# Inverse 640-point stage by residues modulo 5, and slabs 12 and 13 without block products, in a fused spectral-filter and gated-FFN kernel

## The chip, the cores and the metric

One core of a Trainium2 chip. The metric is the device time of one execution in microseconds. TensorE (PE) multiplies matrices into PSUM; VectorE (DVE), ScalarE (ACT) and GpSimd (POOL) do the rest of the arithmetic; SyncE (SP) issues most transfers. Each engine works through its own list of instructions in order and waits on semaphores for the others.

## The reference

```python
xn = layernorm(x)                                   # x: 2048 x 640, bf16
X = rfft2(xn) * (w_r + 1j * w_i)                    # 2048 x 321 frequencies
s = irfft2(X, s=(2048, 640)).astype(bfloat16)
g = silu((gelu(xn @ w_gate) * (xn @ w_up)) @ w_down)  # 640 -> 1536 -> 640
return x + s * g
```

So there are two branches: a spectral filter (a 2048-point transform over the rows, a 640-point one over the columns, both ways) and a gated FFN; their results are multiplied.

## The kernel before

The 2048 rows are cut into 16 slabs of 128 rows (`NS = 16`). Row k of slab n1 is row 16 k + n1, so that the 2048-point transform falls into 128-point matmuls (with `Tfwd`, `Tinv`) and a 16-point part between slabs. The FFN runs over four groups g of four slabs (512 rows).

**What sets the order.** The program is recorded by hand. `back` is the list of backbone pieces, 144 places long; `put(s, f, ...)` hangs a piece of other work behind place s. The engines' lists follow this order. The backbone is the FFN: `ffn_piece` (L809, five matmuls of up to 512 columns, once for the gate, once for the up product; the gate is evacuated by ScalarE as `ge`, L814, and the product by VectorE into `UT`, L816), then the down product. The down product is either direct (`down_third`, L946, 24 matmuls of 320 columns for each slab) or by block products after Strassen and Winograd (`product`, L903, seven products of six matmuls for two slabs, with sums of operands on VectorE in `u_sum`, L884, and sums of results, L910). Groups 1 and 2 (`STR`) use block products throughout; group 3 uses them for its first two slabs, 12 and 13, at places 132 to 137, and the direct form for slabs 14 and 15. The FFN of group 2 ends at place 95, its products take places 96 to 107, the FFN of group 3 places 108 to 131, and its down stage 132 to 143. `gated` applies the SiLU (by ScalarE's table for groups 0 and 3, by a tanh on ScalarE and an operation on VectorE for 1 and 2).

**The spectral branch.** `slab_S1` and `slab_D` transform forward; the result goes through DRAM (`ZDR`) and comes back turned as `B2`. Eleven **bursts** (places 67 to 90, `BURSTS`) do the 16-point parts and the multiplication with the filter: `s2_in` makes `px` with 64 x 64 matmuls (L649), ScalarE copies it to `xs` (L657), VectorE multiplies it by W1 and W2 into `RZ` (L661); `s2_out`, one burst later, makes `pu` (L674), ScalarE copies it in two pieces (L681), even and odd frequencies apart, into a tile that goes to DRAM (`UDR`, L684). A burst covers three of sixteen row pairs and 162 or 159 of the 321 frequencies.

`load_V` (place 91) brings the result back as V, [row, slab, 2 x 321], in two pairs of transfers, slabs 0 to 3 and 4 to 15 (L699). Then, for each slab, `slab_S1i` (L730): five matmuls of 128 columns against `Tinv`, evacuated by one ScalarE copy (L732). Their operands are five blocks of 128 frequencies; four are slices of V, the fifth is put together beforehand by VectorE in `gather` (L709, two copies for a batch of slabs).

**The inverse 640-point stage** takes three slabs as a group (`DG`; the sixth group is slab 15 alone), groups seven places apart. `group_Di` calls `d_group`: for each slab four matmuls of 160 columns on 128 rows (L573) and four of 160 columns on 32 rows, in the four row strips of the array (L577), for the fifth block. It yields sums over even and odd frequencies, real and imaginary. ScalarE evacuates them with their scale (L755, 960 elements), VectorE forms sum and difference of even and odd parts (`group_cs`, L761, two operations), and then the two mirrored halves of the output (`group_Y`, L770 and L772, two operations). `finish` multiplies by the gate (L788), adds x (a transfer with accumulation on POOL's queue for slabs 0 to 11, L790; VectorE for the others, L792) and writes the output (L793).

PSUM: `psB` is two buffers of two banks each, used in turn by px, pu, slab_S1i and the inverse stage; `psA` is two buffers each for `psg` and `psu`.

Of the kernel before, what the change touches and what calls it, by code (L numbers as in the profile page):

```python
# [76 lines left out]
def build(nc, env):  # L77
# [71 lines left out]
    FI = consts.tile([P, 5, LH], BF16)  # L149
# [91 lines left out]
    lint = gtile([LH], INT32)  # L241
    nc.gpsimd.iota(lint, pattern=[[1, LH]], base=0, channel_multiplier=0)
# [10 lines left out]
    ftm = gtile([5, LH], FP32)  # L253
# [49 lines left out]
    kc = []  # L303

    def fwd_consts():
        cq = affine("cq", h_f, -320.0, 320.0)
# [4 lines left out]
        kc.append(cq)  # L311
        ab.extend([(a_m, b_0), (a_m, b_1), (a_m, b_2), (a_m, b_3), (a_y, None)])
# [3 lines left out]
    def inv_consts(part):  # L316
        if part == 0:
            for k, c in enumerate((0.0, 4.0, 2.0)):
                inv_src[k] = affine(f"i_{k}", pf, 4.0, c)
            kc.append(affine("hk", h_f, -2.0, 1.0))  # L320
        else:
            o = [affine(f"o_{k}", pf, 2.0, c) for k, c in enumerate((320.0, 2.0, 321.0, 1.0))]
            i_0, i_1, i_2 = (inv_src[k] for k in range(3))
            ab.extend([(i_0, o[0]), (i_1, o[1]), (i_2, o[2]), (i_2, o[3])])

    def inv_rest():
        cq, hk = kc
        l_s, l_k, l_r, i_r, o_r = (c1(n) for n in ("l_s", "l_k", "l_r", "i_r", "o_r"))
        for out, in0, s1, s2 in ((l_s, s_f, 2.0, 256.0), (l_k, h_f, 2.0, l_s), (l_r, hk, hi_f, l_k),
                                 (i_r, l_r, 2.0, 0.0), (o_r, l_r, 1.0, cq)):  # L330
            nc.gpsimd.tensor_scalar(out=out, in0=in0, scalar1=s1, scalar2=s2, op0=ALU.mult, op1=ALU.add)
        ab.append((i_r, o_r))
# [28 lines left out]
    fv = gtile([10, LH], FP32)  # L361

    def ft_v(g):
        if g < 5:
            parts = [(0, TW, meo[:, g // 2])] if g < 4 else [(0, 66, mys), (66, TW, mys)]
        else:
            parts = [(0, LH, lint)]
# [4 lines left out]
    FW = (TW, LH)  # L372
# [194 lines left out]
    def d_group(lhs, T, w):  # L567
        ps = [psB.tile([P, 2, 512], FP32, tag="b", name=f"pd{b}") for b in range(2)]
        n = len(lhs)
        out = [[ps[g // 2][:, g % 2, a * w:(a + 1) * w] for g in range(4)] for a in range(n)]  # L570
        for a in range(n):
            for g in range(4):
                nc.tensor.matmul(out[a][g], lhsT=lhs[a][:, g, :], rhs=T[:, g, 0:w], start=(a == 0), stop=False)  # L573
        for a in range(n):
            for g in range(4):
                r = slice(32 * g, 32 * g + 32)
                nc.tensor.matmul(out[a][g], lhsT=lhs[a][r, 4, :], rhs=T[r, 4, 0:w], start=False, stop=(a == n - 1))  # L577
        return [t[:, :, 0:n * w].rearrange("p k (a m) -> p a k m", a=n) for t in ps]

# [50 lines left out]
    WB = LH + 1  # L630
    BURSTS = [(h0, 3, l0, w) for h0 in range(0, 15, 3) for l0, w in ((0, WB), (WB, L - WB))]
# [8 lines left out]
    def s2_in(b):  # L640
# [3 lines left out]
        for lo in range(2):  # L644
            r = slice(64 * lo, 64 * lo + 64)
            for hh in range(2):
                for i, j, kind in s2_tiles(b, lo, hh):
# [3 lines left out]
                                     stop=(j == n))  # L651

# [11 lines left out]
    def s2_out(b):  # L664
# [3 lines left out]
        for q, NM in enumerate((N1, N2)):  # L668
            for hh in range(2):
                r = slice(64 * hh, 64 * hh + 64)  # L670
                for lo in range(2):
                    for i, j, kind in s2_tiles(b, lo, hh):
                        ps = pu[64 * lo:64 * lo + 64, hh, i * w:j * w].rearrange("p (h l) -> p h l", l=w)
                        nc.tensor.matmul(ps, lhsT=NM[r, kind, 0:64], rhs=pp[q][r, lo, i:j, :],  # L674
                                         start=(q == 0 and i == 0), stop=(q == 1 and j == n))
        ut = st_b["u"][:, (h0 // 3 + 1) % 2, 0:2 * n, :]
        us = ut.rearrange("p (h k) l -> p k h l", k=2)
        pv = pu[:, :, 0:n * w].rearrange("p k (h l) -> p k h l", l=w)
        for m in range(2):
            c0 = m * LH + l0 // 2  # L680
            nc.scalar.copy(out=us[:, :, :, c0:c0 + (w + 1 - m) // 2], in_=pv[:, :, :, m:w:2])  # L681
        if l0 + w == L:
            for lo in range(2):
                nc.sync.dma_start(out=rows(UDR, lo, h0, h0 + n), in_=turned(ut, lo, 0, n))  # L684
# [5 lines left out]
    VO = (0, L + 1, LH, L + 1 + HD)  # L690
# [13 lines left out]
    def gather(i):  # L704
# [3 lines left out]
        for k, c0, w in ((0, 0, LH), (1, L + 1, HD)):  # L708
            nc.vector.tensor_copy(out=vr.rearrange("p n (b k i) -> p n b k i", b=2, k=2)[:, :, :, k, :],  # L709
                                  in_=V[:, :, c0:c0 + 2 * w].rearrange("p n (b c) -> p n b c", b=2)[:, :, :, P:HD])  # L710
# [30 lines left out]
    eobuf, csbuf = (w1f[:, o:o + 6 * D].rearrange("p (s x) -> p s x", s=2) for o in (4 * D, 10 * D))  # L741

    def quad(buf, i):
        n = DG[i][1]
        return buf[:, i % 2, 0:n * D].rearrange("p (q k a n) -> p q k a n", q=2, k=2, a=n)

    def group_Di(i):
        n0, n = DG[i]
        py = d_group([st_c.pop(n0 + a) for a in range(n)], FI, HD)
        eo = quad(eobuf, i)  # L750
        silu = [(n0 + a) // 4 in BY_SILU for a in range(n)]
        edges = [0] + [a for a in range(1, n) if silu[a] != silu[a - 1]] + [n]
        for b in range(2):
            for a0, a1 in zip(edges, edges[1:]):
                nc.scalar.activation(out=eo[:, b, :, a0:a1].rearrange("p k a n -> p a k n"), in_=py[b][:, a0:a1],  # L755
                                     func=ACT.Copy, scale=(2.0 if silu[a0] else 1.0) / (S * D))

    def group_cs(i, q):
        eo, cs = quad(eobuf, i), quad(csbuf, i)
        flat = "p k a n -> p (k a n)"  # L760
        nc.vector.tensor_tensor(out=cs[:, q].rearrange(flat), in0=eo[:, 0].rearrange(flat),  # L761
                                in1=eo[:, 1].rearrange(flat), op=(ALU.add, ALU.subtract)[q])

    def group_Y(i, q):
        n0, n = DG[i]
        cs = quad(csbuf, i)
        Y = st_c["Y"](n0, n).rearrange("p a (h n) -> p a h n", h=2)
        C, Z = (cs[:, :, k].rearrange("p h a n -> p a h n") for k in range(2))
        if q == 0:
            nc.vector.tensor_tensor(out=Y[:, :, :, 0:HD], in0=C, in1=Z, op=ALU.add)  # L770
        else:
            nc.vector.tensor_tensor(out=Y[:, :, ::-1, 319:159:-1], in0=C, in1=Z, op=ALU.subtract)  # L772
# [65 lines left out]
    def gated(g, j, k, ph, late=False):  # L838
# [19 lines left out]
        else:  # L858
# [5 lines left out]
          for k, b in (((1, 0), XG[:, 0, :]), ((1, 1), RX[:, 0, :]), ((2, 0), XG[:, 0, :]), ((2, 1), SB), ((3, 0), XG[:, 0, :]))}  # L864
# [29 lines left out]
    def product(g, a, i):  # L894
# [12 lines left out]
        if a == 0 and i in (1, 2, 3) and g in STR:  # L907
# [79 lines left out]
    for g in range(4):  # L987
# [76 lines left out]
    for g, at in ((1, 56), (2, 92), (3, 128)):  # L1064
        put(at, u_sum, nc.vector, g, 0, 0, TB)
        if g in STR:
            put(at + 1, u_sum, nc.vector, g, 1, 0, TB)
# [24 lines left out]
    for b in range(len(BURSTS)):  # L1092
        put(sb + AT[b], s2_in, b)
        if b > 0:
            put(sb + AT[b], s2_out, b - 1)
    put(sb + 23, s2_out, len(BURSTS) - 1)
# [3 lines left out]
    for i, at in enumerate((vs0 - 1, vs0, vs0 + 6, vs0 + 15, vs0 + 24)):  # L1100
# [3 lines left out]
    for i, (n0, n) in enumerate(DG):  # L1104
        a = vs0 + 7 * i
# [56 lines left out]
```

## Time and profile before

| | us |
|---|---|
| median of three runs | 196.37 (195.82 to 196.56) |
| the profiled execution, device time | 197.07 |
| its span | 195.2 |
| granted TensorE clock over the span | 1.00 |

The span is the part of the execution in which the engines work; 1.87 us of the profiled execution lie around it. The page gives, for each engine, the busy time and the number of instructions, and a chain of work followed back from the last instruction: whatever released each step is the step before. A group of instructions is shown as line, engine, operation, output <- inputs, shapes and count, then busy us and mean ns of one, then the idle time just before them and what ended it. In a row of the chain stand start, length and what ran. Durations of matmuls overlap, so their rate is read from start to start or from the chain.

### The profile page before, as it was taken

What the parts mean: (1) busy time and instruction counts of PE and PEld (TensorE: products, weight loads), DVE (VectorE), ACT (ScalarE), POOL (GpSimd) and SP (SyncE); (2) the same over time, 40 slices, a digit from 0 to 9 for tenths busy, and PEclk for the clock granted to TensorE, in tenths of its full rate; (3) what the DMA queues carried; (4) which work ended last, traced back from release to release, by engine and by line L of the source; (5) the groups of instructions that cost most, each with busy time, mean ns of one, the idle gap of its engine ahead of it and who ended that gap; (6) DMA issues with size and microseconds to landing.
All of it is one profiled execution on the core that took longest, in us unless ns stands there. A gap on an engine that the chain in (4) does not pass through costs nothing.

```text
span 195.2 us, 4162 instructions
## 1 busy us (share of the span) xinstructions
PE 187.4 (96%) x1496; PEld 115.6 (59%) x1511; DVE 154.5 (79%) x379; ACT 126.6 (65%) x224; POOL 50.5 (26%) x80
## 2 busy tenths in 40 slices
PE   7899999999999999999999999999999999999992
PEld 5788854767555566576533333456765555556772
DVE  7887888989799869899965756587888657587993
ACT  4668567866977877525697787524675757465651
POOL 4448688998030200000000000000003250404100
PEclk9999999999999999999999999999999999999999
DMA  6999999968899999269955233459400836575623
GB/s 167 302 333 358 368 306 170 152 116 259 215 157 175 196 221 230 69 169 234 172 118 116 74 101 101 115 144 288 131 3 2 164 75 150 119 143 125 136 88 85
DMA packets 39989, 32.44 MB, mean 166 GB/s; under 512 B 12960, under 2 KB 38048, under 8 KB 39840
## 3 DMA queue, kind: packets, MB, share of 16 engines
q1 hardware_dynamic: 36176, 27.91, 60.3%
q0 software_dynamic: 1824, 3.28, 10.0%
q10 hardware_dynamic: 1968, 0.98, 1.9%
q8 instruction: 12, 0.20, 0.5%
q14 instruction: 9, 0.07, 0.1%
HBM read 19.03 MB, written 7.88 MB: 138 GB/s over the span
## 4 chain that ended last, share of the span: by engine, by line
PE 80%; DMA 10%; SPq 3%; DVE 3%; ACT 2%; issue 1%; DVEq 0%; ACTq 0%
PE psu L809 25%; PE psg L809 24%; PE psg L946 5%; PE psg L903 4%; PE psu L946 4%; DMA B<-ZDR 4%; PE psu L903 3%; DMA VY<-UDR 2%; PE pz L563 2%; PE pd L573 2%; SPq L624 2%; PE pv L730 2%; PE pd L594 2%; PE pu L674 2%; DMA Tfwd<-Tinv 1%
## 5 line engine op out<-in xcount | busy, mean ns | idle before, releaser
L809 PE MATMUL psu<-XG,Wu 128*128 128x512 bf16 (+2 forms) x285 | 60.4, 342 | 0.4 <-issue 0.3
L809 PE MATMUL psg<-XG,Wg 128*128 128x512 bf16 (+2 forms) x280 | 60.0, 341 | 0.7 <-issue 0.2
L816 DVE TENSOR_TENSOR UT<-psu,ge 128x512 bf16<-128x512 f32 (+2 forms) x58 | 34.4, 594 | 15.1 <-PE psu L809 12.3
L814 ACT ACTIVATE ge<-psg 128x512 bf16<-128x512 f32 (+2 forms) x58 | 30.3, 523 | 23.2 <-PE psg L809 22.5
L809 PEld LDWEIGHTS <-Wu 128*128 128x128 bf16 x290 | 26.1, 98 | 22.5 <-issue 3.4
L809 PEld LDWEIGHTS <-Wg 128*128 128x128 bf16 x290 | 26.5, 98 | 20.2 <-issue 0.2
L790 POOL DMA_DIRECT2D VY<-in_A_x_dram x12 | 10.6, 1035 | 95.3 <-PE psu L809 74.3
L661 DVE TENSOR_TENSOR RZ<-xs,W 128x972 bf16<-128x972 bf16 (+2 forms) x22 | 13.3, 648 | 9.8 <-ACT xs L657 9.5
L903 PEld LDWEIGHTS <-UT 128*128 128x128 bf16 x150 | 14.3, 98 | 6.1 <-issue 0.2
L946 PEld LDWEIGHTS <-UT 128*128 128x128 bf16 x156 | 14.4, 98 | 5.0
L599 ACT CAST RZ<-pd 128x660 bf16<-128x660 f32 x16 | 11.3, 706 | 5.6 <-PE pd L596 5.5
L189 DVE BATCH_NORM_STATS2 st<-X 128x6 f32<-128x320 bf16 x32 | 14.0, 476 | 0.4 <-DMA X<-in_A_x_dram 0.4
L755 ACT ACTIVATE W<-pd 128x960 bf16<-128x960 f32 (+2 forms) x14 | 10.0, 778 | 5.0 <-PE pd L577 5.0
L732 ACT CAST W<-pv 128x640 bf16<-128x640 f32 x16 | 11.0, 688 | 3.3 <-PE pv L730 3.1
L681 ACT CAST RX<-pu 128x486 bf16<-128x486 f32 (+4 forms) x22 | 12.3, 560 | 0.3
L946 PE MATMUL psg<-Wd,UT 128*128 128x320 bf16 (+1 forms) x84 | 11.8, 288 | 0.0
L565 ACT CAST GEN<-pz 128x640 bf16<-128x640 f32 x16 | 11.2, 698 | 0.6 <-PE pz L563 0.6
L657 ACT CAST xs<-px 128x972 bf16<-128x972 f32 (+2 forms) x11 | 10.3, 936 | 1.6 <-PE px L649 1.4
L761 DVE TENSOR_TENSOR W<-W 128x960 bf16<-128x960 bf16 (+1 forms) x12 | 7.0, 599 | 4.3 <-ACT W L755 4.3
L946 PE MATMUL psu<-Wd,UT 128*128 128x320 bf16 (+1 forms) x72 | 10.3, 291 | 0.0
L207 POOL TENSOR_TENSOR rst<-ve,mhalf 128x1 f32<-128x1 f32 (+1 forms) x6 | 5.5, 913 | 11.6 <-DVE ve L205 11.6
L903 PE MATMUL psu<-Wd,UT 128*128 128x320 bf16 x48 | 7.8, 300 | 0.0
(207 smaller groups left out, 295.7 us busy)
## 6 DMA issues: line engine op xcount, KB each, us to landing
ZDR<-RZ SPq DMA_DIRECT2D x16, 160.5 KB, 4.5
UDR<-RX SPq DMA_DIRECT2D x10, 240.8 KB, 3.0
B<-ZDR SPq DMA_DIRECT2D x8, 240.8 KB, 5.2
W<-UDR SPq DMA_DIRECT2D x2, 963.0 KB, 9.4
X<-in_A_x_dram SPq DMA_DIRECT2D x3, 640.0 KB, 10.4
Wd<-in_B_w_down_dram SPq DMA_DIRECT2D x1, 1920.0 KB, 14.7
VY<-in_A_x_dram POOLq DMA_DIRECT2D x12, 160.0 KB, 4.0
out_dram<-VY SPq DMA_DIRECT2D x12, 160.0 KB, 3.1
```

The costliest lines, as they stand in the source:

```text
L189: nc.vector.bn_stats(out=st_n[n1][:, k, :], in_=X[:, n1, 320 * k:320 * k + 320])
L565: nc.scalar.copy(out=Zt[n1], in_=pz)
L599: nc.scalar.copy(out=zd.rearrange("p c (q e) -> p c q e", e=10), in_=pd[:, :, 0:330].rearrange("p c (e q) -> p c q e", q=33))
L661: nc.vector.tensor_tensor(out=pp[-1], in0=xs, in1=WT[:, :, h0:h0 + n, l0:l0 + w], op=ALU.mult)
L681: nc.scalar.copy(out=us[:, :, :, c0:c0 + (w + 1 - m) // 2], in_=pv[:, :, :, m:w:2])
L732: nc.scalar.copy(out=vs, in_=pv)
L790: nc.gpsimd.dma_start(out=Y, in_=xv[:, n1, sl], accum_op=ALU.add)
L809: nc.tensor.matmul(ps, lhsT=WT[:, c, t * P:(t + 1) * P], rhs=xnT[g][:, c, c0:c1_], start=(c == 0), stop=(c == 4))
L814: nc.scalar.activation(out=ges[t], in_=ps, func=ACT.Gelu_apprx_tanh)
L816: nc.vector.tensor_tensor(out=UT[:, t, c0:c1_], in0=ps, in1=ges[t], op=ALU.mult)
L903: nc.tensor.matmul(ps, lhsT=lhs[:, t, :], rhs=rhs[:, t, :], start=(t == 0), stop=(t == 5))
L946: nc.tensor.matmul(ph, lhsT=UT[:, t, j * P:(j + 1) * P], rhs=Wd[:, t, c0:c1_], start=(t == 0), stop=(t == NT - 1))
```

## The change

In the inverse stage the frequencies are now ordered by their residue modulo 10: the copies out of `pu` write each residue as a run of 32 columns, in the order 8, 6, 4, 2, 0, then frequency 320, then 5, 7, 9, 1, 3. The two slices of 128 columns at 0 and at 193 then hold the frequencies that aren't multiples of 5, even and odd, and the 65 between them the multiples of 5. The part of the output that comes from multiples of 5 repeats every 128 columns; the other part sums to nothing over the five positions n, n + 128, ... So the matmuls make 128 instead of 160 columns of each sum, the missing 64 columns of each half are the negated sum of the other four blocks of 64, and the repeating part is added to all five blocks of 128 at the end.

- **Bursts.** Widths 160 and 161. VectorE copies residues 1 and 3 out of `pu` (and frequency 320 in every second burst), ScalarE residues 0 to 8 even and 5, 7, 9 in two copies. VectorE's copy comes ahead of the burst's multiplications, ScalarE's behind the copy of px.
- **Inverse stage.** `group_Di` is gone; `slab_Di` makes five matmuls of 128 columns for each slab, two or more places behind its slab_S1i, and ScalarE evacuates 640 elements. VectorE makes two sums (768 elements for three slabs) and two half outputs (768); `group_rest` is new: VectorE sums blocks twice (768, 384), ScalarE writes the negated sum (384), VectorE adds the repeating part (1920).
- **Order.** Groups are six places apart, gathers stand at places 97, 98, 103, 111 and 120 (97, 98, 104, 113 and 122 before), slab_S1i(0) at 100 (99).
- **Slabs 12 and 13** use `down_third`; their u_sum is gone.
- The constants for the inverse cosines and sines are made from other affine steps, 128 columns each instead of 161.

```diff
-    WB = LH + 1
-    BURSTS = [(h0, 3, l0, w) for h0 in range(0, 15, 3) for l0, w in ((0, WB), (WB, L - WB))]
+    WB = LH
+    BURSTS = [(h0, 3, l0, w) for h0 in range(0, 15, 3) for l0, w in ((0, HD), (HD, WB))]
...
-        for m in range(2):
-            c0 = m * LH + l0 // 2
-            nc.scalar.copy(out=us[:, :, :, c0:c0 + (w + 1 - m) // 2], in_=pv[:, :, :, m:w:2])
+        m, nq = l0 // 10, w // 10
+        for r0, ni, c0, copy in (((1, 2, HD + 97, nc.vector.tensor_copy),),
+                                 ((0, 5, P, nc.scalar.copy), (5, 3, HD + 1, nc.scalar.copy)))[part]:
+            step = -32 if r0 == 0 else 32
+            out = bass.AP(us.tensor, us.offset + c0 + m, [list(us.ap[d]) for d in (0, 2, 1)] + [[step, ni], [1, nq]])
+            src = bass.AP(pv.tensor, pv.offset + r0, [list(pv.ap[d]) for d in (0, 2, 1)] + [[2, ni], [10, nq]])
+            copy(out=out, in_=src)
...
+    def s2_step(b):
+        px = s2_in(b) if b < len(BURSTS) else None
+        pu = s2_out(b - 1) if b else None
+        if b:
+            s2_sort(b - 1, pu, 0)
+        if px is not None:
+            s2_mul(b, px)
+        if b:
+            s2_sort(b - 1, pu, 1)
...
-    def group_Di(i):
+    def slab_Di(n1):
+        i = n1 // 3
+        vs = st_c.pop(n1)
+        pd = psB.tile([P, 5, P], FP32, tag="b", name="pd")
+        for g in range(5):
+            nc.tensor.matmul(pd[:, g, :], lhsT=vs[:, g, :], rhs=FI[:, g, :], start=True, stop=True)
+        nc.scalar.activation(out=parts(eobuf, i, 5)[:, :, n1 - DG[i][0], :], in_=pd, func=ACT.Copy,
+                             scale=(2.0 if n1 // 4 in BY_SILU else 1.0) / (S * D))
...
+    def group_rest(i, q):
+        n0, n = DG[i]
+        Y = halves(i)
+        u = ubuf[:, 0:n * 256].rearrange("p (a h b e) -> p a h b e", h=2, b=2, e=64)
         if q == 0:
+            Yb = Y.rearrange("p a h (b e) -> p (a h) b e", e=64)
+            nc.vector.tensor_tensor(out=u.rearrange("p a h b e -> p (a h) b e"), in0=Yb[:, :, 0:2], in1=Yb[:, :, 4:2:-1],
+                                    op=ALU.add)
+        elif q == 1:
+            nc.vector.tensor_tensor(out=u[:, :, 0], in0=u[:, :, 0], in1=u[:, :, 1, ::-1], op=ALU.add)
+        elif q == 2:
+            nc.scalar.activation(out=Y[:, :, :, P:P + 64], in_=u[:, :, 0], func=ACT.Copy, scale=-1.0)
         else:
+            Yt = st_c["Y"](n0, n).rearrange("p a (t e) -> p a t e", t=5)
+            nc.vector.tensor_tensor(out=Yt, in0=Yt, in1=parts(eobuf, i, 5)[:, 4].unsqueeze(2).to_broadcast([P, n, 5, P]),
+                                    op=ALU.add)
...
-        if g == 3:
-            for k in range(6):
-                back.append((run,) + tuple((product, g, 0, i) for i in range(k * 7 // 6, (k + 1) * 7 // 6)))
-        for j in range(2 if g == 3 else 0, 4):
+        for j in range(4):
...
-    for i, at in enumerate((vs0 - 1, vs0, vs0 + 6, vs0 + 15, vs0 + 24)):
+    for i, at in enumerate((vs0 - 1, vs0, vs0 + 5, vs0 + 13, vs0 + 22)):
         put(at, gather, i)
...
-        a = vs0 + 7 * i
+        a = vs0 + 6 * i
         for k in range(n):
-            put(a + ((1, 2, 4)[k] if n == 3 else 1), slab_S1i, n0 + k)
-        d = a + 6 if n == 3 else a + 4
-        put(d, group_Di, i)
...
+            put(a + (2, 3, 5)[k], slab_S1i, n0 + k)
+            put(a + (4, 6, 7)[k], slab_Di, n0 + k)
+        d = a + (7 if n == 3 else 4)
+        for k, it in enumerate(((group_cs, 0), (group_cs, 1), (group_Y, 0), (group_Y, 1), (group_rest, 0),
+                                (group_rest, 1), (group_rest, 2), (group_rest, 3))):
+            put(min(d + (1, 1, 2, 2, 3, 3, 5, 6)[k], LAST), it[0], i, it[1])
         for k in range(n):
-            put(min(d + (5 + k if n == 3 else 2), vs0 + 41), finish, n0 + k)
+            put(min(d + 7 + k, LAST), finish, n0 + k)
```

More of the change, by code (lines that the diff above doesn't have):

```diff
@@ L565, in slab_S1 @@
         nc.scalar.copy(out=Zt[n1], in_=pz)
[L567 to L578, printed above, removed]
     DG = [(n0, min(3, NS - n0)) for n0 in range(0, NS, 3)]
@@ L758, in group_cs @@
[L758 to L768, printed above, removed]
[L769 to L772 removed]
+        return buf[:, i % 2, 0:g * n * P].rearrange("p (g a n) -> p g a n", g=g, a=n)
```

111 lines of the change are left out of this document (57 added, 54 removed).

## The prediction

> **What bounds the kernel now.** I read the head of the page and its chain of waits, then busy time by stage, then the chain in order of time, and last the timeline and the groups kept apart by shape.
>
> ```profile
> span 195.2 us, 4162 instructions
> PE 187.4 (96%) x1496; PEld 115.6 (59%) x1511; DVE 154.5 (79%) x379; ACT 126.6 (65%) x224; POOL 50.5 (26%) x80
> PE 80%; DMA 10%; SPq 3%; DVE 3%; ACT 2%; issue 1%; DVEq 0%; ACTq 0%
> ```
>
> TensorE is busy 96% of the span and carries 80% of the chain. By stage (busy us follow the length: PE, PEld, DVE, ACT, POOL):
>
> ```profile
> core 0: us, PE busy (x) PEld busy (x) DVE busy (x) ACT busy (x) POOL busy (x), PEclk, DMA share, GB/s
> 97.00:124.00 27.00, 26.18 (x192) 10.35 (x194) 17.19 (x30) 22.31 (x37) 0.00 (x0) 1.00 0.40 93
> 124.00:134.20 10.20, 9.75 (x64) 5.26 (x65) 6.90 (x19) 3.44 (x7) 0.00 (x0) 1.00 0.71 181
> ...
> 145.00:177.30 32.30, 32.01 (x239) 17.52 (x242) 23.25 (x47) 20.26 (x33) 7.94 (x9) 1.00 0.54 109
> 177.30:185.00 7.70, 7.70 (x80) 5.66 (x79) 6.87 (x16) 5.06 (x7) 2.62 (x3) 1.00 0.61 120
> ```
>
> The bursts (97 to 124) and all the inverse stage (from 134) have TensorE full at clock 1.00; only around the loads of V (124 to 134) does it stand, 0.45 us. VectorE has 9 of 32 us free in the middle of the inverse stage. So a matmul removed there is worth its time, as long as the two evacuating engines keep up. The pieces of the chain that price the edits:
>
> ```profile
> 112.42 0.41 PE pu L674 x8
> ...
> 168.69 0.85 PE pd L573 x12
> 169.53 0.32 PE pd L577 x12
> 169.85 0.16 issue
> 170.01 1.03 PE psg L809 x4
> 171.04 1.08 PE psu L809 x5
> ...
> 175.91 0.28 PE pv L730 x5
> ...
> 184.53 0.28 PE pd L573 x4
> 184.81 0.18 PE pd L577 x4
> 184.99 1.74 PE psg L946 x12
> 186.73 1.63 PE psu L946 x12
> ```
>
> **Inverse matmuls.** A group of three slabs costs 0.85 + 0.32 us, and the FFN piece behind it takes 169.85 to 171.04 = 1.19 instead of 1.08: 0.11 more after the 32-row tiles. Together 1.28. The new form is 5 matmuls of 128 columns on full rows for each slab, the shape of one slab_S1i (L730): 0.28, three of them 0.84. Five groups save 5 x 0.44 = 2.2. The last, of one slab, costs 0.28 + 0.18 + 0.11 = 0.57 and will cost 0.28. Term: **-2.5**.
>
> **Slabs 12 and 13.** 7 products of 6 matmuls become 4 x 12 = 48 matmuls of 320 columns, six more at 1.63 / 12 = 0.136. Term: **+0.8**. The VectorE sums that go with the products go too.
>
> **First inverse slab.** slab_S1i(0) moves from place 99 to 100, behind one more product.
>
> ```profile
> 133.03 0.22 PE L730 MATMUL pv<-Tinv,VY 128*128 128x128 bf16 x1
> ...
> 133.59 0.34 PE L730 MATMUL pv<-Tinv,VY 128*128 128x128 bf16 x3 [0.34 <-DMA VY<-UDR]
> ...
> 134.06 0.98 PE L903 MATMUL psg<-X,UT 128*128 128x320 bf16 x6
> ...
> 140.85 0.36 DVE L709 COPY vr<-W 128x256 bf16<-128x256 bf16 x2 [0.32 <-DMA W<-UDR]
> ```
>
> The slab takes 133.03 to 134.06 = 1.03 for work of 0.28: 0.75 of standing, for V (landed near 133.6) and for the gather behind it. With 0.8 of product in front it starts near 133.85. Bounds: 0 gained (if the load slips as much) and 0.75; I take **-0.5**, since the end of the bursts, which releases that load, hardly moves (below).
>
> **The gather that moves up.** gather(2), which waits for the second load of V, goes from place 104 to 103. Counting from 133.85, places 100 to 103 (five products of 0.82, three slabs of 0.28) end near 138.0, so VectorE reaches the gather near 138.5 and stands until 140.85: 2.3 us instead of 0.32. Behind it are queued the product sums, for which ScalarE's tanh waits; behind the tanh stand the evacuations of slab_S1i and slab_Di, and TensorE waits for their two psB buffers. Following the queues place by place, the evacuation of the slab at place 108 ends about 0.4 after TensorE wants that buffer at 110. Bounds: 0 (the buffers cover it) and 2.0 (nothing does). I take **+0.4**, since VectorE is back in step some four places on.
>
> **VectorE and ScalarE in the inverse stage.** Their prices:
>
> ```profile
> L816 DVE TENSOR_TENSOR UT<-psu,ge 128x512 bf16<-128x512 f32 x40 | 27.5, 687 | 13.4 <-PE psu L809 11.1 <-ACT ge L814 1.6 <-issue 0.4
> L814 ACT ACTIVATE ge<-psg 128x512 bf16<-128x512 f32 x40 | 23.9, 597 | 17.1 <-PE psg L809 16.5 <-DVE RX L535 0.3
> L732 ACT CAST W<-pv 128x640 bf16<-128x640 f32 x16 | 11.0, 688 | 3.3 <-PE pv L730 3.1
> L755 ACT ACTIVATE W<-pd 128x960 bf16<-128x960 f32 x8 | 7.3, 968 | 3.4 <-PE pd L577 3.4
> L761 DVE TENSOR_TENSOR W<-W 128x960 bf16<-128x960 bf16 x10 | 6.5, 654 | 4.3 <-ACT W L755 4.3
> L661 DVE TENSOR_TENSOR RZ<-xs,W 128x972 bf16<-128x972 bf16 x10 | 6.2, 665 | 5.3 <-ACT xs L657 5.2
> L816 DVE TENSOR_TENSOR UT<-psu,ge 128x256 bf16<-128x256 f32 x14 | 5.8, 414 | 1.5 <-PE psu L809 1.2 <-ACT ge L814 0.3
> L681 ACT CAST RX<-pu 128x486 bf16<-128x486 f32 x10 | 5.8, 578 | 0.2
> L788 DVE TENSOR_TENSOR VY<-VY,XG 128x640 bf16<-128x640 bf16 x12 | 5.5, 486 | 0.1
> L513 DVE TENSOR_TENSOR GEN<-X 128x1536 bf16<-128x1536 bf16 x3 | 2.9, 954 | 0.0
> L875 DVE TENSOR_TENSOR X<-Wd,X 128x1920 bf16<-128x1920 bf16 x2 | 2.3, 1154 | 0.0
> L884 DVE TENSOR_TENSOR UT<-UT,XG 128x768 bf16<-128x768 bf16 x3 | 1.7, 558 | 1.0 <-PE psu L903 0.9
> L755 ACT ACTIVATE W<-pd 128x320 bf16<-128x320 f32 x4 | 1.6, 432 | 1.6 <-PE pd L577 1.6
> ```
>
> Before, a group of three costs VectorE four operations of 960: 2.6. After: four of 768 (2.23), a sum of 768 (0.56), one of 384 (0.35, between the row of 640 and the slope of these rows), and an add of 1920 in which one operand repeats: 1.15 by L875, and L513, which has such a repeat too, runs at the same rate. Sum 4.3. If no such shape ran at the fast rate, L816 gives the slow one, (687 - 414) / 256 = 1.07 ns an element: 2.2 for the add.
> A group now comes every six places. TensorE needs 6 x 1.08 + 6 x 0.28 = 8.1 for them. VectorE: 3 x 0.69 (L816) + 3 x 0.49 (L788) + 4.3 = 7.8 by durations. Back to back it does better: two multiplications of the bursts take 1.25 (row below) where 2 x 0.665 is 1.33, 0.08 less for an operation that needs nothing of the one before; for eleven of thirteen that leaves 6.9. Hidden, with 1.2 a group to spare, from 67% to about 85% full; if the cover is gone each tenth more costs 0.7 a group. Its last FFN product is late by some 0.7, and the down stage reads that tile twelfth, 1.6 after its start.
> ScalarE: 6 evacuations of 640 (0.69), three gates of 512 (0.60), a negating copy of 384 (between the 0.43 of 320 and the 0.58 of 486, taken 0.48): 6.4 of 8.1, hidden. The negating copy waits for VectorE, with the next gate and evacuations queued behind it: this is where a late VectorE would reach TensorE.
> Towards the end the load falls: products of slabs 12 and 13 took seven sums and seven more on UT from VectorE in 173 to 186. The last slab's finishing and output are as before. Finishing of slab 0 comes three places later, slab 9 at the same place; its transfers have tens of us.
>
> **Bursts.** The timeline of one:
>
> ```profile
> 109.25 0.58 PE L674 MATMUL pu<-RZ,N 64*64 64x477 bf16 x8
> ...
> 110.47 1.17 ACT L681 CAST RX<-pu 128x480 bf16<-128x480 f32 x2
> 110.61 1.25 DVE L661 TENSOR_TENSOR RZ<-xs,W 128x972 bf16<-128x972 bf16 x2 [1.18 <-ACT xs L657]
> ```
>
> TensorE's order and columns (963 a pair of bursts) stay. The frequency sort puts a copy of 192 elements (and one of 6 in every second burst) on VectorE ahead of the multiplications. Bounds 0.1 and 0.41 (L816 with 256); taken 0.33, as the size is nearest. It runs in the 1.18 us in which VectorE waits for ScalarE. ScalarE's two copies become 480 and 288 elements: 0.58 + 0.42 instead of 1.17 (bounds 0.9 and 1.2). They wait for VectorE's copy, which is done while ScalarE copies xs; only after the last burst is there no such copy, up to 0.2 on the loads of V, within the bound above. No DMA is added. Term: **0**. The constants change by a few operations of one column and by 128 for 161 columns, under the FFN's pieces: 0.
>
> **Sum.** -2.5 + 0.8 - 0.5 + 0.4 = -1.8. The profiled execution took 197.07 (span 195.2 and 1.87 around it), so 195.3 there. It lies 0.70 above the median of the runs, 196.37, so **194.6**; with the bounds of the two waits alone 194.3 to 196.7.
>
> **Rivals.** (1) *The late gather eats the gain.* At its upper bound, 2.0 instead of 0.4, the time is 196.2, within 0.5%. For it: everything on ScalarE is in order. Against: VectorE is busy 23 of 32 us just behind, so it recovers.
> (2) *VectorE sets the pace of the inverse stage: slower.* Place: from 108 to the first down piece, four groups. It decides where a group costs VectorE over 8.1. With the 1920 add at 2.2 and the two sums at the slow rate (0.96 + 0.55 for 0.91) the group costs 6.9 + 1.05 + 0.6 = 8.55: 4 x 0.45 = 1.8, and the backlog from the gather, 2.0 - 0.4 = 1.6, is never worked off: 196.37 - 1.8 + 3.4 = 198.0. For it: 85% full, small margins, three orders (reversed, repeated) not seen together. Against: L513 and the reversed writes within L761's family run fast.
> (3) *Odd rows slow the multiplications.* A burst's row is now 161 wide, so rows of xs and RZ begin at odd elements. At the slow rate 966 elements take 0.14 + 966 x 1.07 = 1.17 instead of 0.66: +1.0 a burst. They end at 111.86 and TensorE wants them at 112.42, 0.56 later: 0.45 lost in ten bursts, 199.1. Against: W's rows, 321 long, already begin at odd elements and L661 runs at 0.66.
> [...]
> (4) That it does not do what it says is no case: the instruction order has the fifteen matmuls for each three slabs.
>
> **How the numbers follow.** Forecast 0.56, rival (1) 0.17, (2) 0.22, (3) 0.05. About 0.5% is what a measurement of this kernel tells from no change. Faster is the forecast, 0.56; same is (1), 0.17; slower (2) and (3), 0.27. The forecast's own range is 193.5 to 195.3; to hold eight in ten it must take in (1) and about half of (2): 193.5 to 197.8.
>
> **What would show it.** Right: no 32-row matmuls; 0.28 for each slab_Di; no wait of TensorE at the first slab; VectorE standing about 2 us at the third gather; L644's multiplications near 0.66; VectorE about 85% busy from 145 on with TensorE still full. Wrong: TensorE waiting on psB or psu between places 108 and 132, the 1920 add near 2 us, pu waiting on RZ.

## The result, and the profile after

| | before | after |
|---|---|---|
| median, seven runs each on one chip, us | 196.37 (195.82 to 197.30) | 194.70 (194.57 to 195.27) |
| the profiled execution, us | 197.07 | 195.27 |
| its span, us | 195.2 | 193.5 |

The ratio is 0.9917, with a 95% interval of 0.9889 to 0.9945. The change makes the kernel 1.7 us faster; 194.6 was forecast. The total is right. Of its five terms two are right as they were reckoned, two come out near their size in one execution or another, but by a way that was not the one reckoned, and one left out a loss of 0.25, as the experiments show.

The head of the page of the changed kernel:

```profile
span 193.5 us, 4096 instructions
PE 186.4 (96%) x1453; PEld 115.8 (60%) x1469; DVE 160.7 (83%) x394; ACT 127.4 (66%) x231; POOL 50.8 (26%) x81
PE 92%; DMA 3%; ACT 1%; DVE 1%; issue 1%; SPq 0%
```

By the page TensorE has 43 matmuls fewer and stays 96% busy; VectorE has 15 operations and 6 us more. TensorE's share of the chain of waits has grown from 80% to 92%. Busy time by stage of the changed kernel (columns as in the prediction's table):

```profile
97.00:124.00 27.00, 26.10 (x195) 10.46 (x191) 20.84 (x45) 21.94 (x38) 0.00 (x0) 1.00 0.40 94
124.00:134.20 10.20, 10.15 (x64) 5.48 (x64) 7.98 (x23) 3.50 (x8) 0.00 (x0) 1.00 0.65 171
...
145.00:177.30 32.30, 32.09 (x236) 18.39 (x238) 28.17 (x57) 24.21 (x41) 8.57 (x10) 1.00 0.52 112
177.30:185.00 7.70, 7.70 (x62) 5.64 (x60) 7.49 (x21) 4.28 (x9) 1.98 (x3) 1.00 0.64 133
```

TensorE no longer stands while V is loaded (10.15 of 10.20; 9.75 before). From 145 to 177.3 it is full as before, and VectorE has gone from 23.25 to 28.17 of 32.30, which leaves 4.1, or 1.0 for each of four groups. From 177.3 to 185 VectorE has 0.2 left. The chain of waits, in order of time, has no gap at a slab:

```profile
134.60 0.28 PE pv L735 x5
134.88 0.81 PE psu L926 x6
...
147.96 0.28 PE pd L762 x5
148.24 1.08 PE psu L832 x5
...
177.57 0.28 PE pd L762 x5
...
189.17 0.68 PE psg L969 x12
```

The first inverse slab (L735) takes 0.28 where it took 1.03. Each slab of the new stage (L762) takes 0.28, and the FFN piece behind it starts at once and takes 1.08, without the 0.11 that followed the 32-row tiles. The groups of the changed kernel, kept apart by shape:

```profile
L644 DVE TENSOR_TENSOR RZ<-xs,W 128x960 bf16<-128x960 bf16 x10 | 6.2, 664 | 1.8 <-ACT xs L640 1.6
L644 DVE TENSOR_TENSOR RZ<-xs,W 128x966 bf16<-128x966 bf16 x10 | 6.2, 662 | 1.1 <-ACT xs L640 1.1
L672 ACT CAST RX<-pu 128x480 bf16<-128x480 f32 x10 | 5.9, 591 | 1.6 <-DVE RX L672 1.2 <-ACT xs L640 0.2
L768 DVE TENSOR_TENSOR W<-W 128x768 bf16<-128x768 bf16 x10 | 5.1, 552 | 0.0
L794 DVE TENSOR_TENSOR VY<-VY,W 128x1920 bf16<-128x1920 bf16 x4 | 4.6, 1151 | 0.0
L672 ACT CAST RX<-pu 128x288 bf16<-128x288 f32 x10 | 4.1, 412 | 0.3
L672 DVE CAST RX<-pu 128x192 bf16<-128x192 f32 x10 | 3.6, 356 | 3.3 <-ACT ge L837 1.9 <-PE pu L657 1.3
L791 ACT ACTIVATE VY<-W 128x384 bf16<-128x384 bf16 x4 | 2.1, 514 | 0.0
L789 DVE TENSOR_TENSOR W<-W 128x384 bf16<-128x384 bf16 x5 | 1.8, 358 | 0.2
```

These were not to be seen in the trace of before, and the estimates held: the add with a repeated operand 1151 ns (1.15), the sums 552 and 358 (0.56, 0.35), the sort 356 (0.33), the two copies 591 and 412 (0.58, 0.42), the negating copy 514 (0.48). In both forms of the multiplication (966 and 960 elements) the rows of xs and RZ now lie 161 apart, so that every second one begins at an odd element; they take 662 and 664 ns, and before, 162 apart, 972 elements took 665. Rows that begin at odd elements cost nothing here, in both operands and the output. So rival (3), which put them at 1.17 us, is out.

The third gather (VectorE's timeline of the changed kernel; in brackets the idle time before and its end):

```profile
139.43 0.48 DVE L933 TENSOR_TENSOR XG<-FT,psg 128x320 f32<-128x320 f32 x1
140.52 0.23 DVE L713 COPY vr<-W 128x256 bf16<-128x256 bf16 x1 [0.62 <-DMA W<-UDR]
```

VectorE stands 0.62 there, not 2.3, and in this execution TensorE doesn't wait.

**Where the 1.7 us come from**, by the moments at which TensorE passes the same work in the two profiled executions (after minus before, us): first forward slab +0.33; from the second burst to the fifth (92.79 to 103.02 before, 93.11 to 103.59 after) another +0.25; at the first inverse slab, counted with the product that now stands ahead of it, the work behind it starts at 134.71 against 134.06 + 0.82, so -0.17 in all, that is some -0.75 there; from there to TensorE's end, 189.85 against 191.66 = -1.81, another -1.64; behind that end +0.11. Together -1.70.

### The profile page after: what moved, and what is told of

It is laid out like the page before. It is cut to its first block, busy times and chain, and to the rows that moved or that the text cites. A ratio compares the mean times of both kernels' runs of the same rounds, so it can differ in the third digit from the quotient of the medians.

```text
span 193.5 us, 4096 instructions
## 1 busy us (share of the span) xinstructions
PE 186.4 (96%) x1453; PEld 115.8 (60%) x1469; DVE 160.7 (83%) x394; ACT 127.4 (66%) x231; POOL 50.8 (26%) x81
## 4 chain that ended last, share of the span: by engine, by line
PE 92%; DMA 3%; ACT 1%; DVE 1%; issue 1%; SPq 0%
PE psu L832 27%; PE psg L832 26%; PE psg L969 7%; PE psu L926 6%; PE psg L926 6%; PE psu L969 6%; PE pu L657 2%; PE pz L555 2%; PE pv L735 2%; PE pd L762 2%; PE pd L573 2%; PE px L628 2%; DMA X<-in_A_x_dram 2%; DMA Tfwd<-Tinv 1%; PE pt L996 1%
## 5 line engine op out<-in xcount | busy, mean ns | idle before, releaser
L969 PEld LDWEIGHTS <-UT 128*128 128x128 bf16 x204 | 19.2, 98 | 6.9
L644 DVE TENSOR_TENSOR RZ<-xs,W 128x960 bf16<-128x960 bf16 (+2 forms) x22 | 13.3, 648 | 3.0 <-ACT xs L640 2.7
L969 PE MATMUL psg<-Wd,UT 128*128 128x320 bf16 (+1 forms) x108 | 15.5, 290 | 0.0
L926 PEld LDWEIGHTS <-UT 128*128 128x128 bf16 x120 | 11.4, 98 | 4.6 <-issue 0.2
L969 PE MATMUL psu<-Wd,UT 128*128 128x320 bf16 (+1 forms) x96 | 13.9, 292 | 0.0
L763 ACT ACTIVATE W<-pd 128x640 bf16<-128x640 f32 x16 | 11.1, 700 | 1.7 <-PE pd L762 1.7
L672 ACT CAST RX<-pu 128x480 bf16<-128x480 f32 (+3 forms) x22 | 10.8, 490 | 2.2 <-DVE RX L672 1.2
L640 ACT CAST xs<-px 128x960 bf16<-128x960 f32 (+2 forms) x11 | 10.3, 935 | 1.6 <-PE px L628 1.4
L762 PEld LDWEIGHTS <-W 128*128 128x128 bf16 x80 | 5.8, 98 | 3.1
L672 DVE CAST RX<-pu 128x192 bf16<-128x192 f32 (+1 forms) x11 | 3.9, 350 | 3.9 <-PE pu L657 2.0
```

The costliest lines, as they stand in the source:

```text
L644: nc.vector.tensor_tensor(out=pp[-1], in0=xs, in1=WT[:, :, h0:h0 + n, l0:l0 + w], op=ALU.mult)
L672: copy(out=out, in_=src)
L763: nc.scalar.activation(out=parts(eobuf, i, 5)[:, :, n1 - DG[i][0], :], in_=pd, func=ACT.Copy, scale=(2.0 if n1 // 4 in BY_SILU else 1.0) / ...
L926: nc.tensor.matmul(ps, lhsT=lhs[:, t, :], rhs=rhs[:, t, :], start=(t == 0), stop=(t == 5))
L969: nc.tensor.matmul(ph, lhsT=UT[:, t, j * P:(j + 1) * P], rhs=Wd[:, t, c0:c1_], start=(t == 0), stop=(t == NT - 1))
```

## The experiments

Each was timed in five rounds, the two with more VectorE work in three, beside the kernel before, whose median lay between 196.37 and 196.68. The differences between kernels below are those of the medians; where the ratios, whose runs are taken in pairs, give another figure (times 196.5), both are given, and intervals are those of the ratios. All kernels compute the same but the one of which it is said otherwise.

**The changed kernel again.**

> The changed kernel once more, for comparison with the kernels beside it and to see whether what its first profile lost before the bursts belongs to it. There the first transposes started 0.29 us later than in the kernel before (6.06 against 5.77), behind a later transfer of x, and the first forward slab 0.33 later (41.02 against 40.69); the third burst added 0.25 (0.58 at 101). Theory: the first two are chance of that execution, so here the first transposes start anywhere from 5.7 to 6.1; the 0.25 belongs to the change and stays. Rival: all of it belongs to the change, and the numbers repeat. Time 194.7 by either.

195.05, ratio 0.9921 (0.9898 to 0.9945). In its profile the first forward slab comes at 40.79, 0.10 behind the kernel before (40.69), where the first profile had 41.02: most of that +0.33 is chance of one execution. From the second burst to the fifth it takes 10.47 (10.23 before, 10.48 in the first profile), so the +0.25 belongs to the change.

Behind the bursts this execution isn't like the first. V comes later: the first gather starts at 133.74, after VectorE has stood 0.69 for it (133.45 and 0.17 in the first profile). Slab 0 still doesn't wait, since a product now stands ahead of it, and the step there is again worth -0.73. But further on TensorE waits for a psB buffer, at the third slab_S1i and at the second slab_Di:

```profile
137.49 0.98 PE L926 MATMUL psg<-Wd,UT 128*128 128x320 bf16 x6
138.49 0.38 PE L735 MATMUL pv<-Tinv,VY 128*128 128x128 bf16 x4
```

Six such matmuls take 0.81 from start to start, so slab_S1i is 0.18 late; its buffer is free when ScalarE's copy, behind a tanh that waited for VectorE, ends at 138.44. With the slab_Di that makes 0.37, and from the first slab to TensorE's end the gain is 1.27 instead of 1.64. In the profiles of the kernels below that have this order up to there, it is the same: 0.12 to 0.22 where VectorE stood 0.44 to 0.53 at the first gather, nothing where it stood 0.36 or less.

**The term of the 32-row matmuls.** The kernel before without them, and with the pause that follows them gone; its output lacks the fifth block of frequencies.

```diff
...
-        for a in range(n):
-            for g in range(4):
-                r = slice(32 * g, 32 * g + 32)
-                nc.tensor.matmul(out[a][g], lhsT=lhs[a][r, 4, :], rhs=T[r, 4, 0:w], start=False, stop=(a == n - 1))
```

> The kernel before with the 32-row matmuls of d_group (the fifth block of frequencies) left out: four times five groups of twelve and one of four. Theory, the term of -2.5: what the change saves is these strips and the pause behind them, since 5 matmuls of 128 columns stream as many columns as 4 of 160. 5 x (0.32 + 0.11) + 0.18 + 0.11 = 2.4 us faster than the kernel before, 194.0. Rival, that the strips themselves run beside other matmuls and only the pause counts: 6 x 0.11 = 0.7 faster, 195.7.

194.17, ratio 0.9875 (0.9843 to 0.9907): 2.4 less, as expected. The chain of this kernel:

```profile
167.50 0.85 PE pd L573 x12
168.34 0.05 issue
168.40 1.03 PE psg L805 x4
```

The 160-column matmuls keep their 0.85, which are the new form's 3 x 0.28; what the change saves is the strips and the 0.11 after them. The first term stands.

**The term of slabs 12 and 13**, alone in the kernel before:

```diff
-        if g == 3:
-            for k in range(6):
-                back.append((run,) + tuple((product, g, 0, i) for i in range(k * 7 // 6, (k + 1) * 7 // 6)))
-        for j in range(2 if g == 3 else 0, 4):
+        for j in range(4):
...
-    for g, at in ((1, 56), (2, 92), (3, 128)):
+    for g, at in ((1, 56), (2, 92)):
...
```

> The kernel before with slabs 12 and 13 by the direct down product, nothing else changed: the second term of the sum alone. Theory (TensorE is full there, 7.70 of 7.70): six more matmuls of 320 columns at 0.136, so 0.8 above the kernel before, between 0.5 and 1.1. Rival (the block products with their sums on VectorE held up the end of the kernel before): less than 0.3 above it, or below it.

197.22, ratio 1.0038 (1.0019 to 1.0056): 0.75 to 0.85 more (interval 0.37 to 1.10), as the sum had it. And the other way round, the block products put back into the changed kernel:

> The changed kernel with slabs 12 and 13 by block products again: six matmuls of 320 columns fewer, 0.8 us less of TensorE; VectorE gets back seven sums on UT and seven on the results, some 6 us between places 128 and 137, where its window from 177.3 to 185 is already busy for 7.5 of 7.7 us. Theory that VectorE decides there: TensorE waits for result sums and UT, 1 to 3 us slower than the changed kernel, 195.7 to 197.7. Rival, that TensorE alone counts (the sum of the prediction): 0.8 faster, 193.9.

197.73, ratio 1.0081 (1.0050 to 1.0113): 2.7 to 3.1 more than the changed kernel, where TensorE's work alone would give 0.8 less. Its windows and its waits (who waited for whom: total us, times, longest):

```profile
177.30:185.00 7.70, 5.43 (x42) 3.73 (x41) 7.60 (x21) 3.20 (x5) 2.31 (x3) 1.00 0.61 118
```

```profile
PE psg L969 <- DVE Tfwd L933: 2.1, 1, 2.1
...
PE psu L926 <- DVE FT L933: 1.3, 1, 1.3
```

VectorE, full, holds up the sums of the products' results, and TensorE, with 5.43 of 7.70, waits for them. In the changed kernel the direct form isn't a loss of 0.8 beside the gain: without it, with all else at its place, the gain isn't there.

**The first inverse slab.** First with all slab_S1i one place earlier:

```diff
-            put(a + (2, 3, 5)[k], slab_S1i, n0 + k)
+            put(a + (1, 2, 4)[k], slab_S1i, n0 + k)
```

> The changed kernel with the inverse slabs' first matmuls at the old offsets in their group (one place earlier, slab 0 at place 99). Theory: TensorE stands again at slab 0, for V and the gather, 0.5 to 0.75 us, and nothing else changes: 195.2 to 195.5. Rival, that the wait only moves or is made up later: 194.7, no change.

196.27, ratio 0.9993 (0.9966 to 1.0020): 1.2 to 1.4 more than the changed kernel, but not where it was expected. Slab 0 hardly waits (0.35 in the chain). The chain of this kernel shows the loss in each later group:

```profile
146.80 1.09 PE psg L832 x5
...
148.41 0.51 ACT VY L791
148.93 0.60 ACT W L763
...
149.57 0.44 PE pv L735 x5
```

Behind the piece of 146.80 TensorE has one more FFN piece and a slab_Di, which end at 149.35; slab_S1i starts at 149.57, 0.22 late. One place earlier, slab_S1i falls beside a slab_Di, and the next one needs a psB buffer whose evacuation (L763) stands on ScalarE behind a gate, which follows its FFN piece, and the negating copy (L791). This comes once a group, four times, 0.27 to 0.28 in the other three. It is the way to TensorE that the prediction named for a late VectorE, here brought about by places alone. So the kernel was cleaned of it, with slab 0 alone moved:

```diff
-            put(a + (2, 3, 5)[k], slab_S1i, n0 + k)
+            put(a + (2 if i else 1, 3, 5)[k], slab_S1i, n0 + k)
```

> The changed kernel with slab_S1i(0) back at place 99 and nothing else moved (the three further slabs that came along last time, and met slab_Di, stay). Theory after the profiles so far (V itself lands earlier than before, so that the place is worth little by now): slab 0 takes 0.4 to 0.6 instead of 0.28, and the time is 0.1 to 0.3 above the changed kernel's 195.0. Rival (the place is worth the 0.5 to 0.75 of the term): slab 0 takes about 1.0 and the time is 195.5 to 195.8.

194.80, ratio 0.9921 (0.9901 to 0.9942): the changed kernel's own time. The chain of this kernel:

```profile
132.25 0.81 PE psu L926 x6
133.07 0.28 PE pv L735 x5
133.35 0.81 PE psg L926 x6
```

No stall, at the old place; both stated sizes fell in this run, the smaller one too. V itself lands earlier: the gather of its first batch follows the first issue of its load by 5.30 before (128.34 to 133.64), by 4.21 here (128.47 to 132.68) and by 4.23 in the first profile of the changed kernel (129.22 to 133.45). But in the second profile of the same kernel it is 4.78 (128.96 to 133.74). There a slab at place 99 would start at 133.39 and have its gather only at 134.04, instead of at 133.61 when its fifth matmul is due: an estimated 0.4 of standing, from these rows, which the product in front takes away. So the 0.75 has two parts, the earlier V and the product in front, whose shares differ from one execution to the next; in the times, 194.80 against 195.05, no cost of the old place is seen, but the intervals, 0.8 and 0.9 us wide, would hide 0.4.

In all ten profiles with the new stage the gather follows by 4.21 to 4.78, in three with the old one by 5.09 to 5.30. The transfers are the same in number and size (two of 321 KB and two of 963 KB). What differs in the trace: in three profiles with the old stage a packet of 0.01 MB on the instruction queue q14 comes at 128.8 to 129.0, while V's pair is being issued; in the four with the new stage where it was looked for it comes at 116.6 to 117.6. Tried by shifting SP's list in the kernel before:

```diff
-    nc.sync.dma_start(out=Wd, in_=B_w_down.rearrange("(t p) d -> p t d", p=P))
+    for c in range(0, NT, 2):
+        nc.sync.dma_start(out=Wd[:, c:c + 2], in_=B_w_down.rearrange("(t p) d -> p t d", p=P)[:, c:c + 2])
```

> The kernel before with the load of w_down in six transfers instead of one, nothing else changed: five more instructions on SP's list, long before the loads of V. In three profiles with the old inverse stage one packet of instructions (queue q14) is fetched at 128.8 to 129.0, between the two issues of V's first pair, which take 1.14 to 1.36 and land 3.8 to 3.9 after issue; in the profiles with the new stage that packet comes near 117, the issues take 0.93 and V lands after 3.3 to 3.6. Theory (where SP fetches code decides when V lands): the packet moves ahead of the last bursts, the issues take 0.93, V lands after 3.3 to 3.6, slab 0 takes 0.3 to 0.7 instead of 1.03, and the time is 0.3 to 0.7 below the kernel before. Rival (the load is faster for another reason that belongs to the new stage): V lands after 3.8 to 3.9 wherever the packet is, slab 0 takes 0.9 or more, and the time stays within 0.2.

196.08, ratio 0.9972 (0.9953 to 0.9992): 0.3 to 0.55 less (interval 0.16 to 0.92). The instructions that touch UDR, before (count: shortest/median/longest issue in ns, first and last start):

```profile
L684 SPq DMA_DIRECT2D UDR<-RX x12: 445/542/597, 100.2 to 126.0; - x12
L699 SPq DMA_DIRECT2D VY<-UDR x2: 383/552/721, 128.3 to 128.8; - x2
```

and in this kernel:

```profile
L685 SPq DMA_DIRECT2D UDR<-RX x12: 445/596/978, 100.1 to 126.4; - x12
L700 SPq DMA_DIRECT2D VY<-UDR x2: 380/436/492, 128.8 to 129.2; - x2
```

The packet comes at 126.5 to 127.0. V's pair is now issued as in the changed kernel (longest 492 instead of 721) and the gather follows the first issue by 4.53 (128.75 to 133.28), within the 4.21 to 4.78 of the new stage. But the packet has only moved to the last write of UDR (issued from 125.39 to 127.01), of which one issue takes 978, and the load is issued 0.41 later (128.75 against 128.34); slab 0 takes 0.74 (132.95 to 133.69), 0.29 less than before, and that is where this kernel gains: against the kernel before, TensorE is 0.08 early when slab 0 starts, 0.37 when it is done, and 0.36 when its own work ends. So in this profile V comes sooner with the old stage too, with the packet elsewhere (4.53 instead of 5.09 to 5.30); whether the packet makes up the whole of the difference, the spread between executions leaves open. A kernel before with the packet wholly off that chain was not run.

**Does TensorE set the pace?** The fifth matmul of each slab_Di issued twice:

> The changed kernel with the fifth matmul of each slab_Di issued twice: 16 matmuls of 128 columns more, 16 x 0.056 = 0.9 us of TensorE. Theory, TensorE sets the pace of the whole inverse stage: 0.9 slower, 195.6. Rival, that part of the stage is paced by VectorE or ScalarE and TensorE has room there: under 0.5 slower.

195.83, ratio 0.9961 (0.9947 to 0.9976): 0.8 more, as against the expected 0.9; in the chain each slab takes 0.34 instead of 0.28:

```profile
147.30 0.34 PE pd L763 x6
```

**VectorE's room.** One and two more operations of 1920 elements (1.15) in each group that leave the values as they are:

```diff
+            for _ in range(1):
+                Yf = st_c["Y"](n0, n).rearrange("p a d -> p (a d)")
+                nc.vector.tensor_tensor(out=Yf, in0=Yf, in1=Yf, op=ALU.max)
```

> The changed kernel with one more VectorE operation of 1920 elements for each group (the output's maximum with itself), 1.2 us. How much room VectorE has decides how near rival (2) was. Theory from the prediction, 1.2 us free in a group of 8.1: just hidden, at most 0.5 us slower, 194.7 to 195.2. Rival, that VectorE is already at its limit: each group takes 1.2 longer over four groups, 4 to 5 us slower, 199.

196.01, ratio 0.9977 (0.9954 to 1.0000): 1.0 to 1.1 more, not 0.5 or less. From 145 to 177.3 TensorE is still full, 32.09. The loss comes behind, where the down stage waits for the last product of the FFN:

```profile
PEld L972 <- DVE UT L842: 1.4, 1, 1.4
```

> The same with two such operations, 2.4 us in each group. Theory: 1.2 us free, so 1.2 us too many in each of four full groups, less what the psu buffers and the end of the stage absorb: 2 to 5 us slower than the changed kernel, 196.7 to 199.7, and in the profile TensorE waits for VectorE between places 108 and 132. Rival, that VectorE has far more room (sums that are started back to back cost little): under 1 us slower.

202.93, ratio 1.0333 (1.0283 to 1.0383): 8 more, beyond the expected 2 to 5. Its windows and waits:

```profile
145.00:177.30 32.30, 29.93 (x217) 16.90 (x220) 31.45 (x58) 21.48 (x37) 7.42 (x9) 1.00 0.38 77
177.30:185.00 7.70, 4.42 (x34) 2.63 (x32) 7.60 (x12) 5.09 (x8) 1.45 (x3) 1.00 0.65 152
```

```profile
ACT VY L791 <- DVE W L789: 5.7, 3, 2.1
...
PE pv L735 <- ACT W L763: 3.2, 3, 1.3
```

The second operation costs 7 us where the first cost one: 1.15 a group is just about the room. The way to TensorE is the one foretold, negating copy, evacuation, psB, with 3.2 of waiting in three groups; at the down stage it waits another 2.3 for the last FFN product. And behind that wait its clock is lower: 0.90 granted from 185 to the end at 201.5, after 1.00 in the three stages from 134.2 to 185, and from 184.64 twelve down matmuls take 2.76 in the chain instead of 1.63. So at least 1.1 of the 8 us are not waiting for VectorE itself. So rival (2) is a true mechanism of this kernel; by these two kernels it begins about 1 us a group beyond what the change asks of VectorE.

**The spacing.** Groups seven apart (the last four behind the fifth), gathers at the old places:

```diff
-    for i, at in enumerate((vs0 - 1, vs0, vs0 + 5, vs0 + 13, vs0 + 22)):
+    for i, at in enumerate((vs0 - 1, vs0, vs0 + 6, vs0 + 15, vs0 + 24)):
...
-        a = vs0 + 6 * i
+        a = vs0 + min(7 * i, 32)
```

> The changed kernel with its groups of slabs seven places apart again (the one of slab 15 four behind the fifth), and the gathers at their old places. TensorE's work is the same; VectorE's room in a group grows from about 1.0 to about 2.1 us. Theory (TensorE sets the pace, the spacing is worth nothing in itself): 195.0, between 194.7 and 195.4, TensorE full between 145 and 177.3. Rival (the spacing of six is part of the gain, since it frees the end): the finishing of slabs 12 to 15 is crowded behind the last down pieces, TensorE or the last transfer waits there for VectorE, and the time is 195.7 or more.

195.93, ratio 0.9985 (0.9970 to 0.9999): 0.9 to 1.3 more; the rival held. The chain of this kernel leaves TensorE at 176:

```profile
176.03 0.29 PE pd L762 x5
...
180.01 1.03 DVE W L768 x2
...
185.23 1.17 DVE X L794
```

TensorE isn't late, but the last two groups' sums and the finishing of their slabs run one behind another on VectorE from 180 to the end at 191.4. Six places are needed not for TensorE but to have the longer VectorE work done in time.

**The bursts' 0.25.** VectorE's timelines, before:

```profile
94.76 1.22 DVE L661 TENSOR_TENSOR RZ<-xs,W 128x954 bf16<-128x954 bf16 x2
95.90 0.48 DVE L910 TENSOR_TENSOR Tfwd<-Tfwd,psg 128x320 f32<-128x320 f32 x1
```

and after:

```profile
95.06 0.35 DVE L672 CAST RX<-pu 128x192 bf16<-128x192 f32 x1
95.33 1.23 DVE L644 TENSOR_TENSOR RZ<-xs,W 128x966 bf16<-128x966 bf16 x2
96.48 0.48 DVE L933 TENSOR_TENSOR Tfwd<-Tfwd,psg 128x320 f32<-128x320 f32 x1
```

There is no 1.18 of waiting ahead of these multiplications, those of the second burst: VectorE is still behind with the sums of group 1's products. The sort, 0.27 from start to start, delays them, and the tanh, a gate, the copies and the multiplications of the third burst follow in line. Half of the 0.25 is there when pu of the third burst starts, the other half comes within it: it takes 0.75 in the chain instead of 0.63, since its second half waits for the second multiplication (pu starts at 100.65, the multiplication ends at 100.95, pu's fifth matmul starts at 101.00). So pu does wait for RZ once, one of the signs that the prediction named, though not for odd rows. If that were all, the sort moved to ScalarE in the first two bursts would give the 0.25 back:

```diff
-            copy(out=out, in_=src)
+            (nc.scalar.copy if b < 2 else copy)(out=out, in_=src)
```

> The changed kernel with the first two bursts' copies of residues 1 and 3 on ScalarE instead of VectorE. Theory: in the first bursts VectorE is still behind with the sums of group 1's products, so its copy of 0.36 us is not covered there, as the prediction had it, and delays the tanh on ScalarE and the burst behind it by 0.25; ScalarE stands 0.92 us just then and takes the copy free. The product matmuls behind the third burst then start 0.25 earlier relative to the first FFN piece, 194.45. Rival: ScalarE is the later one there, and its extra copies cost as much: no change or slower.

194.90, ratio 0.9927 (0.9905 to 0.9948), no change, and from the second burst to the fifth it takes 10.57. ScalarE's timeline of this kernel:

```profile
97.94 0.32 ACT L672 CAST RX<-pu 128x192 bf16<-128x192 f32 x1
98.15 0.97 ACT L640 CAST xs<-px 128x960 bf16<-128x960 f32 x1
```

The sort, a third copy out of pu, now stands ahead of xs, for which VectorE waits. Both engines are in arrears there; it is the copy more, not its engine. That reading is argued from the timelines; a kernel without a third copy was not run.

## Why the prediction came out right, point by point

- **Inverse matmuls, -2.5.** Right: 2.4 by the kernel without strips, 0.28 for every slab_Di in the chain. That TensorE sets the pace there, on which it rests, is shown by the matmul issued twice.
- **Slabs 12 and 13, +0.8.** Right: 0.75 to 0.85 alone, and -1.64 for this and the term above together in the first profile and in the second without its waits, where the sum had -1.7.
- **First inverse slab, -0.5.** Somewhat small (-0.75 and -0.73), and right in its reason only in part. The step that failed is the assumption that the load of V keeps its place behind the bursts: V came 0.3 to 1.1 sooner after its issue, with a packet of instructions that comes at 128.8 to 129.0 in the one code and near 117 in the other. Where it came soonest, slab 0 doesn't wait at the old place either, and the product in front is worth nothing; in the second profile of the changed kernel it is worth an estimated 0.4. Neither the diff nor the order shows that; the trace of before did, in one packet that I didn't read.
- **Late gather, +0.4.** 0 in the first profile and 0.37 in the second, but not at the third gather. The way is the one described, evacuations behind ScalarE's tanh and TensorE short of a psB buffer; it starts at the first gather, when V is late. At the third VectorE stood 0.62 and 0.18, not 2.3, and the first of TensorE's waits (138.49) comes ahead of it (140.38). The step "VectorE reaches the gather near 138.5" was 1.4 too early (139.9 in the first profile). The count left out the slab_Di at place 102, 0.28, and the later start and bursts, 0.58; the rest is VectorE's own delay. And the load ended at 140.5, not 140.85. (The count's 138.0 comes out from 133.03; 133.85 already holds the first of the five products.) Rival (1), 2.0 at that gather, goes with it.
- **Bursts, 0.** Wrong: +0.25. The timeline shown was that of a late burst, where VectorE waits 1.18; the second burst has no such cover.
- **VectorE and ScalarE in the inverse stage, hidden.** Right, and closer than stated: 1.0 to spare a group instead of 1.2. One more operation of 1920 used it up, and two cost 8 us: more than the 198.0 of rival (2), which was of the right kind with a fair chance.
- **The sum.** First profile: -2.5 + 0.8 - 0.75 + 0 + 0.25 = -2.2; with +0.33 from the start and +0.11 behind TensorE's end it gives the span's -1.7. Second profile: -2.5 + 0.8 - 0.73 + 0.37 + 0.24 = -1.8, with +0.10 and +0.06 the span's -1.6. The forecast had -1.8. What V's arrival costs or doesn't cost in an execution, and how late the start is, decide between these; the medians' -1.7 (by the ratio's interval -1.1 to -2.2) doesn't tell them apart. That the forecast fell within 0.1 of the median is partly luck: it had 0.25 too little gain at the slab and left out a loss of 0.25 in the bursts, and its +0.4 came from the wrong gather. Its lower bound with the two waits, 194.3, doesn't follow from the bounds given either: -2.5 + 0.8 - 0.75 from 196.37 is 193.9.

## What to carry to other kernels

Matmuls on a quarter of the rows cost more than a quarter here, where TensorE was full: twelve on strips of 32 rows took 0.32 us, twelve of as many columns on 128 rows 0.85, and with the 0.11 that came behind them the strips made 0.43 of 1.28 us a group. Removing them paid to the full, 2.4 us. But the exchange has a second half: it gave VectorE 5 us more in 32 and used its room almost up, so that dropping the block products and closing up the groups, which look like a cost and like a detail, are what makes the gain possible. Cover shown in one round of a loop must be looked for in the first rounds too, when other work is still in arrears. And a wait read in one profile, or its absence, should be looked up in a second one of the same kernel before a term is called right or wrong.

## What was not expected of the hardware

The place of one packet of instructions, 0.01 MB on queue q14, goes with the time of a transfer that other engines wait for. With it at 128.8 to 129.0, V's first gather comes 5.09 to 5.30 us after the first issue of its load, and one issue of V's pair takes 721 ns in the kernel before, where the longest takes 492 in the changed kernel. With it at 126.5 to 127.0 the gather comes after 4.53 us, and an issue of UDR's last write takes 978 ns, where the longest of that line takes 597 in the kernel before. With the new stage the gather comes after 4.21 to 4.78. That the packet is SyncE's is my reading: one load split in six at the start of SyncE's list, with nothing else changed, moved it, and made the kernel before 0.3 to 0.55 us faster.

In the kernel with two added operations a wait of TensorE of 2.3 us is followed by a granted clock of 0.90 from 185 to the end at 201.5; in the one with the block products put back, a wait of 2.1 is followed by 1.00 from 185 to the end at 196.4. What makes the difference isn't shown.
